# Masking the value product's blocks in one packed VectorE step, with ScalarE and GpSimd spreading the parts

## The chip, the cores and the metric

The kernel runs on one core of a Trainium2 chip. The metric is the device time of one execution in microseconds (us). The median of three runs of the kernel before is 414.5 us (413.69 to 414.89). The profile is of one more execution.

The core's engines are TensorE (PE in the profile, with PEld for its weight loads), VectorE (DVE), ScalarE (ACT), GpSimd (POOL) and SyncE (SP), whose queue starts most of the DMA transfers. Each works through its own list of instructions in order, and they wait for each other by semaphores.

## The reference

One block of a network: a layer norm, then linear attention with 32 heads of 16 columns, and beside it a two-layer MLP on the same normalised rows; both results and the input are added. What matters here, with `S = 2048` rows and `D = 512`:

```python
xn = _layernorm(x)
q, k, v = split(xn @ wqkv)                 # 32 heads of 16 columns
pq, pk = phi(q), phi(k)                    # phi(t) = where(t > 0, t + 1, exp(t)) + 1e-6
kv  = einsum("bhsd,bhse->bhde", pk, v)     # one 16x16 block per head
z   = einsum("bhsd->bhd", pk)
num = einsum("bhqd,bhde->bhqe", pq, kv)
den = einsum("bhqd,bhd->bhq", pq, z) + 1e-6
attention = (num / den) @ wo
r = relu(xn @ w1 + b1)
out = x + attention + (r * r) @ w2 + b2
```

Everything is float32. The change concerns `kv`, of which only the 32 diagonal blocks of 16x16 exist.

## The kernel before

**Float32 in parts.** Nearly every matrix operand is written as a high part (a copy rounded to the type that TensorE takes, `fp32r`) and a low part (the operand less its high part). `split(h, l, src, eh, el)` (line 117) makes them: a copy on engine `eh`, line 111 when that is ScalarE, and then a subtraction on engine `el`, line 119. A product of two such operands is three matmuls: high by high, high by low, low by high (`PASSES`, line 124; `three`, line 127, matmuls at line 130; `product`, line 480, matmuls at line 484).

**The stages.** Rows are worked in tiles of 128 and bands of four tiles. First a loop over the 16 tiles normalises them, turns them, projects the keys, applies `phi`, and sums in four PSUM banks the product of the normalised rows and `phi(k)` (`kx`, line 385). After that, the kernel computes queries and MLP for two bands at a time, in two rounds (`n` at line 915); each round has a loop over steps `p` (line 1040) that works a fast matrix multiplication out of sums and differences of blocks (the tiles `T`, `S` and `aop`). The tiles `m` hold the attention matrix: per head the `kv` block times the rows of `wo`.

**The order.** Nothing is scheduled automatically: the order in which the program text issues instructions is the order on each engine. The hand-written tables `AT` and `AE` say where delayed steps go. DMA loads are held back until the buffer that they fill is released by the engine that reads it.

**The step that is changed** stands between the two stages. `values()` (line 879, called at line 969) multiplies the value weights `wvs` with `kxs` in 128 small matmuls of 32 columns (line 889). Each lands on 32 partitions, so that the bank `pkv` holds 16 blocks of 32x32, packed: partition group `g` (32 partitions) and column group `j` (32 columns) hold the block of columns `128 j + 32 g`. Such a block covers two heads, and only its two 16x16 diagonal blocks are wanted; `heads` is the mask, made on GpSimd at the start (lines 531 to 536) as a 128x128 matrix with ones in the 16x16 blocks on the diagonal.

What the attention matrix needs is a block-diagonal operand: for each `j`, 128 rows by 128 columns, with the block of group `g` at rows and columns `32 g`. So the tile `kv` (128x512) is cleared by GpSimd (line 882), and four VectorE steps (line 894, one for each `g`) multiply the packed blocks on 32 partitions by the mask and write them to their places. Then `kvt`, its high and low part, is made from the whole of `kv`, zeros included: a ScalarE copy of 128x512 (line 111) and a VectorE subtraction of 128x512 (line 119).

`kvt` is the stationary operand of `matrix(j)` (line 900), three matmuls for each `j`, into the banks `pm`. `matrix(0)` and `matrix(1)` are called at lines 1123 and 1124 in step `p = 0` of the first round, ahead of the third of its products; `matrix(2)` and `matrix(3)` follow at lines 1159 and 1187. Around `values()`, VectorE also makes the low parts of `aop` (line 119), `T` and `w2r` (line 122) and the block sums `S` (line 714), and adds products into `q` (lines 1073, 1161, 1053). ScalarE makes the high parts (line 111). The raw rows of `w2` come by DMA (line 206), and GpSimd copies parts of them (`w2r`, `w2q`, lines 210 and 214).

## Time and profile before

| | us |
|---|---|
| median of three runs | 414.5 |
| the profiled execution | 413.35 |
| its span, from the first to the last instruction | 411.6 |
| TensorE busy | 406.3 |
| VectorE busy | 311.2 |
| ScalarE busy | 264.9 |
| GpSimd busy | 58.7 |

The clock that TensorE was granted is 1.0 of full speed over the whole span.

In the profile a row of a timeline gives the start, the duration, the engine, the line of the program, the instruction, the tile written and the tiles read, the shape (partitions x elements) and how many neighbouring instructions of a kind are put together; in brackets stands how long the engine was idle before and what ended that. A matmul's row is longer than the distance to the next one, since matmuls overlap: the distance of the starts tells what one costs. Tile names come without their numbers: `b` stands for all four banks of the products, `aop`, `T` and `S` for their operands, `pm` for the banks of `matrix`, and `w2r` and `r` for the parts and the raw rows of `w2`.

### The profile page before, as it was taken

Reading aid. Unit: us, or ns where it says so; the run is one execution under the profiler, and the core shown is the slowest. Engines: PE = TensorE matmul, PEld = TensorE weight load, DVE = VectorE, ACT = ScalarE, POOL = GpSimd, SP = SyncE. Lnnn points to the kernel's source line nnn. Section 1 sums busy time; section 2 is a strip of 40 time slices with the busy share of each in tenths; the row PEclk is TensorE's granted clock in tenths of the full one; section 3 lists DMA queues with packets and bytes.
Section 4 is the critical chain, followed back from the end, with each engine's and each line's share of the span. In section 5 each row is a group of like instructions: output and inputs, shape, how many; then the busy total and the mean of one; then the engine's idle time right before and its main releaser. Section 6 shows DMA issues by size and latency. Waiting matters only on the chain.

```text
span 411.6 us, 5590 instructions
## 1 busy us (share of the span) xinstructions
PE 406.3 (99%) x1927; PEld 334.0 (81%) x1927; DVE 311.2 (76%) x558; ACT 264.9 (64%) x465; POOL 58.7 (14%) x92
## 2 busy tenths in 40 slices
PE   8999999999999999999999999999999999999996
PEld 7788888888878888888878888888888888878885
DVE  5885666797899898988449995567989686449843
ACT  4666677656768779788638631577588857737520
POOL 4442333220310000030000130100000200001210
PEclk9999999999999999999999999999999999999999
DMA  6969672810422221273366992411121871024502
GB/s 213 343 217 337 195 307 103 246 36 0 118 64 68 87 76 52 79 201 55 133 239 236 401 166 90 116 51 53 51 76 29 236 186 37 0 101 156 102 2 102
DMA packets 45662, 55.16 MB, mean 134 GB/s; under 512 B 8001, under 2 KB 29761, under 8 KB 44354
## 3 DMA queue, kind: packets, MB, share of 16 engines
q1 hardware_dynamic: 43330, 50.61, 37.1%
q0 software_dynamic: 2304, 4.20, 6.3%
q8 instruction: 15, 0.25, 0.2%
q14 instruction: 13, 0.11, 0.1%
HBM read 41.43 MB, written 13.37 MB: 133 GB/s over the span
## 4 chain that ended last, share of the span: by engine, by line
PE 70%; DVE 3%; issue 1%; ACT 0%
PE acc L130 37%; PE b L484 30%; PE acc L495 2%; DVE T L122 1%; PE b L130 1%; PE pz L130 1%; DVE aop L119 1%; PE acc L502 0%; DVE S L714 0%; DVE w2r L122 0%; PE end L130 0%; DVE kvt L119 0%; ACT kvt L111 0%; DVE q L1053 0%; DVE q L1161 0%
## 5 line engine op out<-in xcount | busy, mean ns | idle before, releaser
L130 PE MATMUL acc<-w2r,s 128*128 128x512 f32 x477 | 112.8, 390 | 0.0
L130 PEld LDWEIGHTS acc<-w2r,s 128*128 128x128 f32 x477 | 89.4, 188 | 19.2 <-issue 0.7
L484 PE MATMUL b<-T,aop 128*128 128x512 f32 x336 | 84.0, 390 | 0.4 <-ACT T L111 0.2
L484 PEld LDWEIGHTS b<-T,aop 128*128 128x128 f32 x336 | 62.8, 188 | 14.7 <-ACT T L111 0.6
L385 PE MATMUL kx<-pk,tok 128*128 128x512 f32 x192 | 46.5, 391 | 0.1
L385 PEld LDWEIGHTS kx<-pk,tok 128*128 128x128 f32 x192 | 35.8, 188 | 7.9 <-ACT pk L111 0.5
L1021 POOL DMA_DIRECT2D res<-in_B_b_dram x16 | 14.4, 1089 | 180.5 <-DVE dt L426 64.2
L484 PE MATMUL b<-xs0h,aop 128*128 128x512 f32 x112 | 36.9, 390 | 0.0
L130 PE MATMUL acc<-mh,aTsr 128*128 128x512 f32 x112 | 35.6, 389 | 0.0
L1029 DVE TENSOR_TENSOR res<-acc,res 128x512 f32<-128x512 f32 x16 | 11.0, 692 | 23.1 <-PE acc L130 18.5
L119 POOL TENSOR_TENSOR tok<-xp,tok 128x512 fp32r<-128x512 f32 x16 | 20.7, 1298 | 43.4 <-ACT tok L111 43.4
L122 DVE TENSOR_TENSOR w2r<-r,w2r 128x512 fp32r<-128x512 f32 (+2 forms) x35 | 25.6, 734 | 0.1
L111 ACT ACTIVATE aop<-S 128x512 fp32r<-128x512 f32 x28 | 17.5, 624 | 11.7 <-DVE S L714 11.7
L484 PEld LDWEIGHTS b<-xs0h,aop 128*128 128x128 f32 x112 | 21.0, 188 | 4.4
L130 PEld LDWEIGHTS acc<-mh,aTsr 128*128 128x128 f32 x112 | 21.0, 188 | 4.4
L119 DVE TENSOR_TENSOR aop<-S,aop 128x512 fp32r<-128x512 f32 x28 | 19.5, 698 | 4.8 <-ACT aop L111 4.4
L119 DVE TENSOR_TENSOR s<-c,s 128x512 fp32r<-128x512 f32 x20 | 13.6, 690 | 11.0 <-ACT s L111 11.0
L484 PE MATMUL b<-xs0l,aop 128*128 128x512 f32 x56 | 21.8, 389 | 0.0
L130 PE MATMUL acc<-ml,aTsr 128*128 128x512 f32 x56 | 21.8, 389 | 0.0
L111 ACT ACTIVATE w2r<-r 128x512 fp32r<-128x512 f32 x32 | 19.6, 619 | 2.3 <-DMA out_dram<-res 2.0
L111 ACT ACTIVATE T<-Tf 128x512 fp32r<-128x512 f32 x16 | 9.5, 626 | 16.4 <-DVE Tf L657 16.1
L484 PE MATMUL b<-xs1h,aop 128*128 128x512 f32 x56 | 19.5, 389 | 0.0
(196 smaller groups left out, 765.0 us busy)
## 6 DMA issues: line engine op xcount, KB each, us to landing
r<-in_B_w_dram SPq DMA_DIRECT2D x49, 256.0 KB, 3.0
res<-in_A_x_dram SPq DMA_DIRECT2D x8, 512.0 KB, 4.6
res<-in_B_b_dram POOLq DMA_DIRECT2D x16, 256.0 KB, 5.5
out_dram<-res SPq DMA_DIRECT2D x15, 256.0 KB, 2.0
via<-xp SPq DMA_DIRECT2D x5, 512.0 KB, 3.0
xg<-via SPq DMA_DIRECT2D x20, 128.0 KB, 2.6
xTd<-t SPq DMA_DIRECT2D x8, 256.0 KB, 4.4
x<-in_A_x_dram SPq DMA_DIRECT2D x4, 512.0 KB, 8.1
```

Of the source, the lines that this page charges most:

```text
L111: nc.scalar.activation(o, i, AF.Copy, bias=bias)
L119: ENG[el].tensor_tensor(out=l, in0=src, in1=f32(h), op=OP.subtract)
L122: nc.vector.tensor_tensor(out=l, in0=src, in1=f32(h), op=OP.subtract)
L130: nc.tensor.matmul(ps, lhsT=a[u], rhs=b[v], start=first and n == 0, stop=last and n == 2)
L385: nc.tensor.matmul(kxp[c], lhsT=tok[i][:, u, c * P:(c + 1) * P], rhs=pk[i][:, v], start=i == 0 and (u, v) == first, stop=i == NT - 1 and ( ...
L484: nc.tensor.matmul(ps, lhsT=a[u][:, j * P:(j + 1) * P], rhs=b[v][:, j, :], start=first and j == 0 and n == 0, stop=last and j == 1 and n == 2,
L495: nc.tensor.matmul(ps, lhsT=s[u][:, k * P:(k + 1) * P], rhs=w2s[NF - 1][u][:, a:z], start=first and u == 0, stop=stop and u == 1)
L1021: nc.gpsimd.dma_start(r[:, i], b2[None, :].partition_broadcast(P), accum_op=OP.add)
L1029: nc.vector.tensor_tensor(out=r[:, a:z], in0=ps, in1=r[:, a:z], op=OP.add)
```

## The change

`values()` no longer writes the masked blocks to a cleared 128x512 tile. One VectorE step multiplies the packed 128x128 product by the mask, which is repeated over the four column groups, and leaves it packed. For that the mask's four 32x32 diagonal blocks have to lie in the first 32 columns: three small GpSimd copies at the start put them there. The cleared tile is now `kvt` itself, 128 partitions by 1024 elements, in two halves for the high and the low part. For each group of 32 partitions, ScalarE copies the four blocks into their places in the high half, and GpSimd subtracts and writes the low half. The VectorE subtraction over 128x512 is gone.

```diff
@@ -534,6 +534,9 @@
                                 pattern=[[-sign * (D // H), P * H // D], [0, D // H]],
                                 channel_multiplier=sign)
+    for k in range(1, NJ):
+        rows = slice(32 * k, 32 * (k + 1))
+        nc.gpsimd.tensor_copy(heads[rows, :32], heads[rows, rows])
     groups = {}
@@ -878,8 +881,9 @@
     def values():
         ps = bank("pkv", "acc")
-        t = w512("kv", "p", 6)
-        nc.gpsimd.memset(t, 0.0)
+        t = w512("kv", "p", 6)[:, :P].rearrange("p (j d) -> p j d", j=NJ)
+        kvt[0] = work.tile([P, 2, 512], F32R, name="kvt", tag="r3")
+        nc.gpsimd.memset(f32(kvt[0]), 0.0)
         R = 32
@@ -889,13 +893,12 @@
+        nc.vector.tensor_tensor(out=t, in0=ps[:, :P].rearrange("p (j d) -> p j d", j=NJ),
+                                in1=heads[:, None, :R].to_broadcast([P, NJ, R]), op=OP.mult)
         for g in range(NJ):
             rows = slice(R * g, R * (g + 1))
-            nc.vector.tensor_tensor(out=t[rows].rearrange("p (j d) -> p j d", j=NJ)[:, :, rows],
-                                    in0=ps[rows, :P].rearrange("p (j d) -> p j d", j=NJ),
-                                    in1=heads[rows, rows][:, None, :].to_broadcast([R, NJ, R]), op=OP.mult)
-        kvt[0] = work.tile([P, 2, 512], F32R, name="kvt", tag="r3")
-        split(kvt[0][:, 0], kvt[0][:, 1], t, "act", "dve")
+            h, l = (kvt[0][rows, u].rearrange("p (j d) -> p j d", j=NJ)[:, :, rows] for u in range(2))
+            split(h, l, t[rows], "act", "pool")
```

## The prediction

> **What bounds the kernel now.** I read the page first, then the busy time in stretches, then the chain of waits, then each engine's timeline around the change. All times are microseconds from the start of the span.
>
> The first fence is from the page: busy time, and the chain that ended last by engine.
>
> ```profile
> PE 406.3 (99%) x1927; PEld 334.0 (81%) x1927; DVE 311.2 (76%) x558; ACT 264.9 (64%) x465; POOL 58.7 (14%) x92
> ...
> PE 70%; DVE 3%; issue 1%; ACT 0%
> ```
>
> TensorE (PE) is busy for 99% of the span, so a change elsewhere earns only what PE now waits. Where is that? I cut the span into stretches (length, then busy time and count of PE, PEld, DVE, ACT, POOL):
>
> ```profile
> 103.50:119.70 16.20, 15.79 (x90) 12.32 (x76) 14.77 (x27) 11.41 (x23) 4.42 (x6) 1.00 0.40 116
> 119.70:408.20 288.50, 288.49 (x1283) 237.54 (x1283) 220.28 (x398) 187.05 (x326) 19.71 (x22) 1.00 0.38 112
> ```
>
> From 119.70 to 408.20 PE never waits: 288.49 of 288.50. In the stretch before it, which holds the changed step, VectorE (DVE) is busy 14.77 of 16.20. The chain of waits runs there:
>
> ```profile
> 104.57 1.91 issue
> 106.47 0.64 ACT kvt L111
> ...
> 107.14 0.69 DVE kvt L119
> ...
> 108.35 1.02 DVE aop L119 x2
> 109.37 1.01 DVE w2r L122
> ...
> 117.11 0.60 DVE q L1161
> 117.71 1.20 DVE T L122 x2
> 118.91 0.61 DVE q L1053
> ```
>
> So from 104.6 to 119.5 the chain is DVE's queue, and from 119.66 it is PE to the end. What PE loses in that stretch can be read from its starts:
>
> ```profile
> 107.86 1.53 PE L130 MATMUL pm<-wo,kvt 128*128 128x512 f32 x6
> 109.23 1.53 PE L484 MATMUL b<-T,aop 128*128 128x512 f32 x6
> ...
> 117.23 0.39 PE L484 MATMUL b<-xs0h,aop 128*128 128x512 f32 x1
> 117.86 1.63 PE L484 MATMUL b<-T,aop 128*128 128x512 f32 x6 [0.24 <-ACT T L111]
> 119.66 1.63 PE L484 MATMUL b<-T,aop 128*128 128x512 f32 x6 [0.17 <-DVE q L1053]
> 121.12 1.98 PE L495 MATMUL acc<-w2r,sz 128*128 128x512 f32 x8
> ```
>
> Six matmuls take 109.23 − 107.86 = 1.37, or 0.228 each. From 117.23 to 117.86 stands 0.63 where one matmul needs 0.23: 0.40 lost. From 117.86 to 119.66 stands 1.80 where six need 1.37: 0.43 lost. From 119.66 to 121.12 it is 1.46: 0.09 lost. **The cap on any gain downstream of the changed step is thus about 0.9 us**, however much DVE saves.
>
> **The change part by part.** It touches DVE, ScalarE (ACT) and GpSimd (POOL) between 105.2 and 108.7. DVE's timeline:
>
> ```profile
> 105.21 1.18 DVE L894 TENSOR_TENSOR kv<-pkv,heads 32x128 f32<-32x128 f32 x4
> 107.14 0.69 DVE L119 TENSOR_TENSOR kvt<-kv,kvt 128x512 fp32r<-128x512 f32 x1 [0.75 <-ACT kvt L111]
> 107.75 0.68 DVE L122 TENSOR_TENSOR T<-Tf,T 128x512 fp32r<-128x512 f32 x1
> 108.35 0.41 DVE L119 TENSOR_TENSOR aop<-rq,aop 128x256 fp32r<-128x256 f32 x1
> 108.69 0.68 DVE L119 TENSOR_TENSOR aop<-S,aop 128x512 fp32r<-128x512 f32 x1
> ```
>
> *DVE, removed:* three of the four L894 products (1.18 / 4 = 0.295 each), the idle 0.75 before the low part of kvt, and that subtraction, 0.61 to the next start. The new product has 128 columns over 128 partitions. The bounds are 0.295 (the same 128 columns on 32 partitions) and 0.41 (256 columns on all); I take the former, for its column count. So L894 ends at 105.50 and the T subtraction starts at about 105.45 and not 107.75: 2.3 earlier.
>
> *ACT:* one copy of 512 columns becomes four of 128.
>
> ```profile
> 106.47 0.63 ACT L111 ACTIVATE kvt<-kv 128x512 fp32r<-128x512 f32 x1 [1.91 <-issue]
> 107.01 0.40 ACT L111 ACTIVATE aop<-rq 128x256 fp32r<-128x256 f32 x1
> 107.32 0.61 ACT L111 ACTIVATE aop<-S 128x512 fp32r<-128x512 f32 x1
> ...
> 108.32 0.62 ACT L111 ACTIVATE w2r<-r 128x512 fp32r<-128x512 f32 x1
> ```
>
> Start to start, 512 columns take 0.52 and 256 take 0.31, so 128 take about 0.205 (ends 0.1 and 0.31), and one lasts 0.30. The first starts 0.08 after L894, as now, at 105.58; the four end at 105.88, 106.09, 106.29 and 106.50. The copy of aop<-rq starts at 106.40 (was 107.01) and aop<-S at 106.71: ACT gains 0.61. The w2r copy would come at 107.71 but needs its load. SP's timeline, and the DMA view of the same moments:
>
> ```profile
> 105.52 1.05 SPq L206 DMA_DIRECT2D r<-in_B_w_dram  x2
> ```
> ```profile
> r<-in_B_w_dram SPq DMA_DIRECT2D x2, 64.0 KB, 2.0
> ```
>
> The second of these begins about halfway, at 106.05, and lands 2.0 later, at about 108.1. It was released by a DVE step ahead of the change, so it doesn't move. So w2r starts at 108.1 and not 108.32, and ends at 108.72: **ACT keeps only 0.2 of its 0.61**. The low part of w2r on DVE (now 109.37 in the chain) then starts at about 108.78: a DVE gain of 0.5 to 0.6 survives that point. Of it the PE gaps at 117.86 and 119.66 can return 0.40 and then the rest.
>
> *POOL, added:* four subtractions of 32x128, each behind its ACT copy. No such row exists. The neighbours, from the groups by form and from POOL's timeline:
>
> ```profile
> L119 POOL TENSOR_TENSOR tok<-xp,tok 128x512 fp32r<-128x512 f32 x16 | 20.7, 1298 | 43.4 <-ACT tok L111 43.4
> ...
> L115 POOL CAST w2q<-w2r 32x512 fp32r<-32x512 f32 x4 | 3.5, 875 | 0.2
> ```
> ```profile
> 4.61 0.24 POOL L241 TENSOR_SCALAR y<-mv 128x1 f32<-128x1 f32 x1 [2.22 <-DVE mv L231]
> ```
>
> Lower end: a quarter of 1.30, 0.32. Upper end: 0.88, the w2q casts, POOL's only steps on 32 partitions. Taken: a fixed part of 0.24 (a step on a single column) and a quarter of the remaining 1.06: 0.50, and some 0.05 less from start to start, 0.45. I choose it for being nearest to tok's row, the same operation.
>
> When is the low part due? PE's weight loads of that product (matrix 0) and where they now stand:
>
> ```profile
> 107.86 0.42 PEld L130 LDWEIGHTS pm<-wo,kvt 128*128 128x128 f32 x2
> ```
>
> Each product makes three passes, high, high, low; the second of these two loads, one matmul spacing (0.23) behind the first at 108.09, is the first that needs the low part. Now it is ready at 107.83, 0.26 early. If PE waits here, everything on it moves by that wait, less the gaps of 0.9.
>
> *POOL beside DVE.* Two pairs of rows show what happens when both are busy; first POOL's, then DVE's of the same moments, a step with two SBUF inputs:
>
> ```profile
> 84.69 1.33 POOL L119 TENSOR_TENSOR tok<-xp,tok 128x512 fp32r<-128x512 f32 x1 [2.98 <-ACT tok L111]
> ```
> ```profile
> 84.79 1.78 DVE L679 TENSOR_TENSOR wv<-wv,wvl 128x512 f32<-128x512 f32 x1
> ```
> ```profile
> 109.90 3.66 POOL L115 CAST w2q<-w2r 32x512 fp32r<-32x512 f32 x4
> ```
> ```profile
> 112.04 2.06 DVE L122 TENSOR_TENSOR T<-Tf,T 128x512 fp32r<-128x512 f32 x2
> ```
>
> The DVE step that began 0.1 behind POOL took 1.78 and not 0.69: it ended 0.55 after POOL's did. In the second pair the DVE steps take 1.03 each and the casts 0.88 each: they alternate. So a new subtraction can hold up DVE, or wait for it. The T subtraction holds to about 106.06, so the first new one starts there (its ACT copy is ready at 106.02). Without any DVE step between, the four end at 106.06 + 3 × 0.45 + 0.50 = 107.9. DVE's next step, aop<-rq, is ready at 106.87 and takes 0.34 from POOL: 108.25. With the aop<-S step (0.61) let in too: 108.86. To this comes about 0.14, as now from w2r's end (108.94) to POOL's start (109.08). Due at 108.09, PE waits 0, 0.3 or 0.9. I take one step let in, 0.3: aop<-S becomes ready only when most of POOL's work is done.
>
> The Trainium skill, "SBUF — State Buffer", section "SBUF: two separate sides", says the same more strictly: the pair of ports is an exclusive lock for a whole instruction, against a DVE step with two SBUF inputs; this trace's 1.78 agrees. "GPSIMD Engine Reference", section "Engine selection", speaks against the change: two-input elementwise work is about twice as slow there as on VectorE. By that page a subtraction would be an estimated 0.59 (twice 0.295) and the low part would come some 0.4 later than by my 0.45 spacing; the 1.30 against 0.69 of this trace bears the ratio out.
>
> *Covered edits.* The cleared tile is now kvt, 1024 columns and not 512, and POOL can do it once the last tok step has ended:
>
> ```profile
> 96.14 0.53 POOL L882 MEMSET kv<- 128x512 f32 x1 [4.94 <-DVE pk L373]
> 109.08 0.76 POOL L115 CAST w2r<-w2r 64x512 fp32r<-64x512 f32 x1 [12.42 <-ACT w2r L111]
> ```
>
> It costs about 1.06 inside idle times of 4.9 and 12.4: nothing. The three copies of head blocks stand ahead of POOL's step at 4.61, before which it sits idle for 2.22. A copy's row:
>
> ```profile
> 8.24 0.18 POOL L591 COPY x<-xp 128x1 f32<-128x1 f32 x1
> ```
>
> Three at 0.18 to 0.32 (the quarter above) make 0.5 to 1.0, under the 2.22; without this cover they would delay the first tile by as much.
>
> **Sum.** DVE's queue reaches the end of the stretch 0.5 to 0.6 earlier; PE itself could come 0.9 − 0.3 = 0.6 earlier. The later of the two decides: a gain of 0.5. The profiled execution took 413.35 (span 411.6 and 1.75 around it), so 412.85; it lies 1.15 below the median of 414.5, so on the median **414.0**.
>
> **Rivals.** *All gaps close (413.6).* POOL's pieces overlap or cost 0.32, PE never waits for kvt, and w2r's load lands early enough: gain 0.9. For it: 0.40 and 0.43 are real gaps behind DVE. Against: the load at 108.1.
>
> *The wait moves to POOL (414.5).* Two DVE steps are let in, the low part is ready at 109.0, PE waits 0.9 and the gaps it had later pay for it: no gain, 414.3 to 414.8. For it: the strict alternation around 110 to 113. This is where the skill's exclusive lock leads if DVE's steps are always waiting. Against: DVE waits for ACT until 106.87.
>
> *The small subtractions are slow (415.3), the other side.* At the 0.88 of the w2q casts, the last ends at 106.06 + 3.5 = 109.6, is seen at 109.7, and PE stands 1.6 to 1.7 where it stood 0; the gaps give 0.9 back: 0.8 slower. It is slower from the point at which the low part comes after 109.0. If DVE is held as well and the gaps stay, up to 1.7: 416.2. Against: those casts had four times the columns and DVE's full steps in between.
>
> **How the numbers follow.** Forecast (gain of 0.3 to 0.7: 413.8 to 414.2) 0.45; all gaps close (413.4 to 413.8) 0.15; the wait moves (414.3 to 414.8) 0.28; slow subtractions (415.2 to 416.2) 0.12. The range from 413.3 to 415.2 leaves out the last and little more; its ends take in the 0.6 by which the three runs scatter about their median. A change of under 0.3%, 1.24 us, is about what a measurement of this kernel cannot tell from none. Faster by that exceeds the cap of 0.9: 0.04, for scatter alone. Slower by that, above 415.74, is half of the last case: 0.06. Within it: 0.90.
>
> **What would show it.** L894 as one step near 0.29; four ACT copies 0.2 apart; the T subtraction near 105.45; w2r's copy waiting for a DMA to 108.1; kvt's last subtraction ending near 108.2; the first pm product's third weight load at 108.1 to 108.6; the gaps at 117.2 and 119.2 shorter. The forecast is wrong if PE waits over 0.9 for kvt, if DVE's gain is lost to POOL before 117, or if PE shows idle time after 121 that it doesn't show now.

## The result, and the profile after

| | before | after |
|---|---|---|
| median (22 executions each) | 413.81 (412.80 to 414.95) | 412.88 (412.11 to 414.76) |
| the profiled execution | 413.35 | 412.76 |
| its span | 411.6 | 411.1 |

The ratio is 0.9978, with a 95% interval of 0.9968 to 0.9987: the change makes the kernel 0.9 us faster (0.54 to 1.32). The forecast was 414.0, in a range from 413.3 to 415.2, so the time lies below the range. Two things put it there. The forecast started from a median of three, 414.5, where 22 executions give 413.81; and it gave the change 0.5 where 0.9 was measured.

The page shows VectorE 1.0 less busy and GpSimd 3.8 more:

```profile
PE 406.3 (99%) x1927; PEld 334.4 (81%) x1927; DVE 310.2 (75%) x554; ACT 265.7 (65%) x468; POOL 62.5 (15%) x99
```

VectorE's timeline after, around the change (start, duration, engine, line, operation, tiles, shape, and in brackets its idle time and what ended it):

```profile
105.06 0.28 DVE L896 TENSOR_TENSOR kv<-pkv,heads 128x128 f32<-128x128 f32 x1
105.26 0.68 DVE L122 TENSOR_TENSOR T<-Tf,T 128x512 fp32r<-128x512 f32 x1
107.20 0.43 DVE L119 TENSOR_TENSOR aop<-rq,aop 128x256 fp32r<-128x256 f32 x1 [1.27 <-ACT aop L111]
...
108.72 1.71 DVE L122 TENSOR_TENSOR w2r<-r,w2r 64x512 fp32r<-64x512 f32 x2 [0.23 <-ACT w2r L111]
```

The packed product takes 0.28, the T subtraction starts at 105.26 and not at 107.75, and VectorE is now idle for 1.27 and 0.23 waiting for ScalarE. It reaches the low part of `w2r` at 108.72, where it was queued until 109.29 before. ScalarE's timeline of the same moments:

```profile
105.42 1.31 ACT L111 ACTIVATE kvt<-kv 32x128 fp32r<-32x128 f32 x4 [1.01 <-issue]
106.75 0.42 ACT L111 ACTIVATE aop<-rq 128x256 fp32r<-128x256 f32 x1
...
107.60 0.58 ACT L111 ACTIVATE c<-b 128x512 f32<-128x512 f32 x1
108.08 0.62 ACT L111 ACTIVATE w2r<-r 128x512 fp32r<-128x512 f32 x1
```

The four copies stand (106.75 − 105.42) / 4 = 0.33 apart. The `w2r` copy follows `c<-b` by 0.48, as it did before (107.84 to 108.32), and its row names no wait. GpSimd's row for the low part:

```profile
105.81 2.14 POOL L119 TENSOR_TENSOR kvt<-kv,kvt 32x128 fp32r<-32x128 f32 x4 [13.64 <-ACT kvt L111]
```

The low part of `kvt` is complete at 105.81 + 2.14 = 107.95, with the pieces 0.53 apart. The three copies of `heads` (0.70 together, at 2.47) and the clearing of `kvt` (0.95, at 91.22) stand far ahead of it. TensorE's timeline:

```profile
107.70 1.53 PE L130 MATMUL pm<-wo,kvt 128*128 128x512 f32 x6
109.07 1.53 PE L484 MATMUL b<-T,aop 128*128 128x512 f32 x6
...
117.05 0.39 PE L484 MATMUL b<-xs0h,aop 128*128 128x512 f32 x1
117.28 1.61 PE L484 MATMUL b<-T,aop 128*128 128x512 f32 x6
119.08 1.63 PE L484 MATMUL b<-T,aop 128*128 128x512 f32 x6 [0.19 <-DVE q L1056]
```
```profile
120.55 1.99 PE L495 MATMUL acc<-w2r,sz 128*128 128x512 f32 x8
```

From 107.70 to 109.07 stand 1.37 for six matmuls: TensorE does not wait for `kvt`. From 117.05 to 117.28 stand 0.23, so the first gap of 0.40 is closed. From 117.28 to 119.08 stand 1.80 for six, as before: the second gap, 0.43, is still there. The chain of waits runs through VectorE's queue from `w2r` to this addition:

```profile
108.72 0.68 DVE w2r L122
...
118.33 0.61 DVE q L1056
```

To compare profiles whose starts are shifted, I use the **stage**: the time from the start of the `pkv` matmuls to the start of those of L495. Before it runs from 102.35 to 121.12, 18.77; after from 102.20 to 120.55, 18.35. So the change earns 0.42 here. Of the 0.59 between the two profiled executions the other 0.15 lies ahead of the stage (102.35 against 102.20); in five profiles of the unchanged kernel the first matmul of `pkv` starts anywhere from 101.85 to 102.86, so that part is scatter.

The 0.42 has a history on VectorE. Counted from the start of `pkv`, it reaches the low part of `w2r` 0.41 earlier than before, at 6.53 and not at 6.94. There its two steps take 1.71 where they took 2.11: before, GpSimd's cast of `w2r` had started first (109.08 against 109.29), and now VectorE's step does (108.72 against 108.83). The same two cases stand in every profile in which the order can be seen: 2.11 to 2.13 in the five where GpSimd starts first, 1.71 in the twelve where VectorE does. So VectorE is 0.81 ahead at its next addition (8.27 and not 9.08). Then it meets one more of GpSimd's `w2q` casts, which end at the same 113.6 as before, and gives 0.41 back. The low part of `aop` after, and then before:

```profile
113.04 1.09 DVE L119 TENSOR_TENSOR aop<-r,aop 128x512 fp32r<-128x512 f32 x1
```
```profile
114.03 0.68 DVE L119 TENSOR_TENSOR aop<-r,aop 128x512 fp32r<-128x512 f32 x1
```

Behind the stage the 0.42 is kept. The first matmuls of `acc<-w2r,s` (L130), some 12 behind those of L495, start 30.37 after those of `pkv` before (132.72 − 102.35) and 29.94 after (132.14 − 102.20), 0.43 less. I call this the **long stage**; from its end to the end of the span every profile of either kernel and its variants takes 278.9.

The 22 executions say more than 0.42, however. Over many executions those of the kernel before pile up around 412.9 and around 414.1, with fewer between. Here and below I call those above 413.5 late and count them. In the kernel before 16 of 22 do, and 102 of the 155 that were timed beside all the runs of this study; in the changed kernel 3 of 22, and 5 of 34 with its second measurement. A fixed mark favours a kernel that is faster throughout: moved down by the stage's 0.42 it counts 9 of the 34, which is still far fewer. The medians of the executions up to 413.5 are 413.20 and 412.82, 0.38 apart, near the stage's 0.42. The rest of the 0.9 is that late executions became rarer. What the late ones lose is the second question of the experiments.

### The profile page after: what moved, and what is told of

It reads as the page before. It is cut to its first block, busy times and chain, and to the rows that moved or that the text cites. A ratio compares the mean times of both kernels' runs of the same rounds, so it can differ in the third digit from the quotient of the medians.

```text
span 411.1 us, 5600 instructions
## 1 busy us (share of the span) xinstructions
PE 406.3 (99%) x1927; PEld 334.4 (81%) x1927; DVE 310.2 (75%) x554; ACT 265.7 (65%) x468; POOL 62.5 (15%) x99
## 4 chain that ended last, share of the span: by engine, by line
PE 92%; DVE 3%; ACT 2%; DMA 1%; issue 1%; POOL 0%; POOLq 0%
PE acc L130 37%; PE b L484 30%; PE pk L365 11%; PE kx L385 10%; PE acc L495 2%; PE pz L130 1%; DVE T L122 1%; PE b L130 1%; DMA x<-in_A_x_dram 1%; PE pt L304 1%; DVE aop L119 0%; DVE w2r L122 0%; ACT kxs L111 0%; ACT aop L111 0%; PE acc L502 0%
## 5 line engine op out<-in xcount | busy, mean ns | idle before, releaser
L130 PE MATMUL acc<-w2r,s 128*128 128x512 f32 x477 | 112.8, 390 | 0.0
L130 PEld LDWEIGHTS acc<-w2r,s 128*128 128x128 f32 x477 | 89.4, 188 | 19.3 <-issue 0.7
L130 PE MATMUL acc<-mh,aTsr 128*128 128x512 f32 x112 | 35.6, 389 | 0.0
L130 PEld LDWEIGHTS acc<-mh,aTsr 128*128 128x128 f32 x112 | 21.0, 188 | 4.4
L130 PE MATMUL acc<-ml,aTsr 128*128 128x512 f32 x56 | 21.8, 389 | 0.0
```

The lines of the kernel that those rows point to most:

```text
L130: nc.tensor.matmul(ps, lhsT=a[u], rhs=b[v], start=first and n == 0, stop=last and n == 2)
```

## The experiments

The theory after the result: VectorE's chain, from the low part of `w2r` to the additions into `q`, sets when TensorE gets past the two gaps, and the change brings it there 0.42 earlier. The rivals: the low part of `kvt` on GpSimd has become a limit; the GpSimd work at the start matters; the pieces' sizes are set by the spread destination; and, for the late executions, several causes that are taken up below. Each set of runs was timed on one chip beside executions of the kernel before, and the ratios compare within a set.

### The kernels again, as controls

c1_before is the unchanged kernel run as if it were a change, d1_after the changed one a second time; e4_before, f3_before and f4_before are single profiled executions of the kernel before.

> The kernel before, once more, timed against itself. Ratio 1.000; its interval shows what five rounds can tell. In its profile the two gaps of TensorE in the stage behind the value product stand as before: 0.63 us between the starts of the last b<-xs0h matmul and the first b<-T one (0.40 lost), and 1.80 us over the six b<-T matmuls (0.43 lost). If the first row statistics start at another time than 3.61, the whole trace is moved by that, and a part of the 0.5 us between the two spans was start-up scatter.

> After, once more. Theory A (VectorE's earlier arrival closes the first gap of 0.40 and nothing else): 0.4 to 0.6 us faster than before, ratio 0.9985 to 0.9990. Theory E (both kernels stand at the w2r copy when its rows land late; what a pair of runs shows depends on that landing): the ratio scatters from set to set between 0.996 and 1.000, and in the profile the addition q<-b,c of line 1164 follows the end of ScalarE's w2r copy by the same 7.7 to 7.8 us as in after (116.45 - 108.70).

> One more look at the kernel before. Its time is in one of two clusters, 412.6 to 413.3 or 413.9 to 414.5. Theory E: in the upper cluster ScalarE's w2r copy waits for a DMA and stage pkv to L495 takes about 20 us, in the lower one 18.8. If it is in the upper cluster with 18.8, the difference between the clusters lies elsewhere.

> A look at the kernel before, to catch a late execution. Theory E: if the time is above 413.5 us, ScalarE's w2r copy waits for a DMA and pkv to L495 takes 19.5 to 20.1 us. Otherwise the loss stands ahead of the value product, as the 1.16 us in e3_best for a transfer of x.

> The same once more: above 413.5 us with a wait of the w2r copy for a DMA (theory E), or with a loss elsewhere.

The control gave 1.0011 (0.9989 to 1.0034). The second measurement of the changed kernel gave 0.9973 (0.9955 to 0.9991), a median of 412.65, and a stage of 18.35 again. E4 took 412.89 with a stage of 18.79: an on-time execution has the same stage as the profile of before, to 0.02 (and a long stage of 30.39 beside 30.37). The profiles of c1 (414.28), f3 (414.08) and f4 (415.72) caught late executions, with stages of 20.09, 19.92 and 20.57. In c1, ScalarE's row and then TensorE's rows show what is late:

```profile
109.53 0.63 ACT L111 ACTIVATE w2r<-r 128x512 fp32r<-128x512 f32 x1 [1.54 <-DMA r<-in_B_w_dram]
```
```profile
113.72 1.67 PE L484 MATMUL b<-T,aop 128*128 128x512 f32 x6 [0.62 <-ACT c L111]
118.75 1.63 PE L484 MATMUL b<-T,aop 128*128 128x512 f32 x6 [0.53 <-ACT T L111]
120.55 1.63 PE L484 MATMUL b<-T,aop 128*128 128x512 f32 x6 [0.17 <-DVE q L1053]
```

ScalarE waits 1.54 for the raw rows of `w2`, everything behind it on ScalarE and VectorE is late, and TensorE pays for it in three places: the stage is 1.32 longer. F3 and f4 show the same: waits of 1.38 and 2.01 ahead of this copy. (F4 is late in a second place too: `pkv` starts at 102.86, 1.0 later than in e4.) The view of the loads gives the reason. In c1 the two loads of 64 KB take 3.7 from issue to landing where they took 2.0 in the profile of before:

```profile
r<-in_B_w_dram SPq DMA_DIRECT2D x2, 64.0 KB, 3.7
```

### What is left of the second gap

c2_sum_first takes the changed kernel and issues the addition of `t5` into `q` (L1056) ahead of VectorE's low parts of `T`, which TensorE doesn't need as soon.

```diff
-                last_sums(4, difference_high, difference_low)
+                last_sums(4, difference_high)
...
                 nc.vector.tensor_tensor(out=t5 if was == "w" else q[t2][:, pb], in0=before, in1=t5, op=OP.add)
+            if p == 1:
+                last_sums(4, difference_low)
```

> After, and the two low parts of the fourth sum T are made behind the addition of t5 on VectorE instead of ahead of it. Theory A (VectorE's queue releases TensorE's banks): the second gap closes too, since the addition q<-b,t ends 1.2 us earlier; six b<-T matmuls take 1.37 to 1.45 us and not 1.80, and the time falls by 0.35 to 0.45 us below after: ratio to before 0.9968 to 0.9978 if after is at 0.9978 by 0.9 us, 0.998 if after's own gain is the 0.42 of its stage. Rival B (TensorE waits there for the low parts or for ScalarE's sz): no change against after.

TensorE's rows:

```profile
116.96 0.39 PE L484 MATMUL b<-xs0h,aop 128*128 128x512 f32 x1
117.45 2.97 PE L484 MATMUL b<-T,aop 128*128 128x512 f32 x12
```

The twelve matmuls stand together, so the second gap is gone, and it was a matter of VectorE's order; 0.26 of the first came back (117.45 − 116.96 − 0.23). In this profile ScalarE waits 0.18 for the rows of `w2`, and VectorE comes to `w2r` 0.30 later than in the changed kernel (6.83 behind the start of `pkv`, and not 6.53). The stage is 18.19, 0.16 under the changed kernel's, where theory A had 0.35 to 0.45. None of it arrives: the long stage is 30.25 (132.31 − 102.06), 0.31 over the changed kernel's 29.94, about as much as those rows came late. The median of 413.01, with a ratio of 0.9982 (0.9964 to 1.0000), doesn't tell it from 412.88. So by this profile closing the second gap by another order earns nothing in the end.

### Is the low part on GpSimd the limit?

c3_low_dve gives the four low parts to VectorE; c4_low_thrice makes each of them three times on GpSimd.

```diff
-            split(h, l, t[rows], "act", "pool")
+            split(h, l, t[rows], "act", "dve")
```
```diff
             split(h, l, t[rows], "act", "pool")
+            nc.gpsimd.tensor_tensor(out=l, in0=t[rows], in1=f32(h), op=OP.subtract)
+            nc.gpsimd.tensor_tensor(out=l, in0=t[rows], in1=f32(h), op=OP.subtract)
```

> After, with the four low parts on VectorE and not on GpSimd. Theory A: VectorE waits for ScalarE's four copies (to 106.7) and is then 1.8 us later at the T subtraction than after, but it makes up most of that, as it then waits less for aop and w2r; its additions into q come 0.2 to 0.4 us later than in after, the first gap stays closed or nearly, the second grows: 0.1 to 0.4 us slower than after, 0.1 to 0.4 faster than before. Rival C (the gain is the leaving of VectorE altogether, so it is all lost): 0.4 to 0.5 slower than after, equal to before.

> After, with each low part made three times on GpSimd: twelve subtractions of about 0.52 us and not four, so that the last ends near 112 and not at 107.96. It shows what a late low part costs. Theory A: TensorE stands at the first product of matrix(0) from 107.9 until 112, about 4 us, and the gap of 0.43 that is left later gives at most that back: 3.2 to 4.0 us slower than after (ratio to before 1.006 to 1.0075). Rival D (TensorE finds other work or the wait is short, as the low part is used late): under 1 us.

C3 was expected to be 0.1 to 0.4 slower than the changed kernel, and it was not: median 412.89, ratio 0.9982 (0.9965 to 0.9999), stage 18.37, long stage 29.97. Its VectorE timeline says why:

```profile
105.71 1.29 DVE L119 TENSOR_TENSOR kvt<-kv,kvt 32x128 fp32r<-32x128 f32 x4 [0.42 <-ACT kvt L111]
...
108.68 1.71 DVE L122 TENSOR_TENSOR w2r<-r,w2r 64x512 fp32r<-64x512 f32 x2
```

The 1.29 that VectorE spends here it spent waiting in the changed kernel; it comes to `w2r` at 108.68 either way. So **the GpSimd half of the change earns nothing here**. What earns is on VectorE: one product of 0.28 in place of four of 1.18 together, and a wait of 0.42 in place of 0.75, against which the four low parts cost 1.29 where one of 0.69 stood.

C4 shows what it costs when the low part does come late. GpSimd's last piece ends at 113.73; TensorE's rows:

```profile
113.79 2.07 PE L130 MATMUL pm<-wo,kvt 128*128 128x512 f32 x4 [5.78 <-POOL kvt L903]
115.66 2.76 PE L484 MATMUL b<-T,aop 128*128 128x512 f32 x6
```

The ratio is 1.0174 (1.0138 to 1.0210) at a median of 420.82, twice the loss that was expected. The first four of GpSimd's twelve pieces start 0.53 to 0.62 apart, later ones up to 1.05, where they alternate with VectorE's steps. And TensorE, once it has its operand, is slow: the six matmuls from 115.66 take 2.56, to the start of the next ones at 118.22, and not 1.37. In the busy time by stretch (length, then busy time and count of PE, PEld, DVE, ACT and POOL, then the granted clock) it stands directly:

```profile
113.70:119.40 5.70, 5.61 (x14) 4.41 (x15) 2.13 (x6) 2.65 (x6) 3.07 (x6) 0.52 0.00 1
```

After 5.78 idle the clock is 0.52 of full speed for about 5.5. The rule for that stands in the Trainium skill, "TensorE: Matmul & The Clock Gate", section "What's actually happening": after an idle window of about 3.4 us the array gets half its clock, until it has been busy for at least one such window. The 0.52 agrees.

### What a piece costs by itself

d4_pieces computes nothing of the reference: it copies one tile of `x` to the output and beside that times blocks of 128 columns on ScalarE and GpSimd, eight of each kind one behind the other: on all partitions (`whole`), on one group of 32 (`same`), on groups that change from one to the next (`turns`), and with the destination spread over the four blocks, on one group (`still`) or on changing ones (`spread`).

```diff
+    for k in range(8):
+        act(same[one(k), k, :P], src[one(k), :P])
+    for k in range(8):
+        act(turns[group(k), k, :P], src[group(k), :P])
...
+    for k in range(8):
+        sub(gturns[group(k), k, :P], src[group(k), :P], low[group(k), :P])
```

> The costs by themselves: it computes nothing of the reference and writes a part of x over the whole output. Eight ScalarE copies of 128 columns each: on 128 partitions; on partitions 0 to 31; on the four groups of 32 in turn; into four blocks of 32 columns on one group; and so on the groups in turn, as in the change. Then the same on GpSimd as subtractions. Forecast's theory: 0.205 us from start to start on ScalarE in all. Rival F: copies that change the group of partitions don't overlap and take 0.33. Rival G: it is the spread destination that takes 0.33. GpSimd: 0.45 start to start in all by the forecast; 0.53 was seen in after.

Both engines' rows from the timeline:

```profile
5.54 1.69 ACT L71 ACTIVATE whole<-src 128x128 fp32r<-128x128 f32 x8
7.13 1.69 ACT L71 ACTIVATE same<-src 32x128 fp32r<-32x128 f32 x8
7.46 3.32 POOL L86 TENSOR_TENSOR gsame<-src,low 32x128 fp32r<-32x128 f32 x8
8.73 2.52 ACT L71 ACTIVATE turns<-src 32x128 fp32r<-32x128 f32 x8
10.75 3.98 POOL L86 TENSOR_TENSOR gturns<-src,low 32x128 fp32r<-32x128 f32 x8
11.26 1.70 ACT L71 ACTIVATE still<-src 32x128 fp32r<-32x128 f32 x8
12.87 2.52 ACT L71 ACTIVATE spread<-src 32x128 fp32r<-32x128 f32 x8
14.79 3.98 POOL L86 TENSOR_TENSOR gspread<-src,low 32x128 fp32r<-32x128 f32 x8
```

Take one duration (0.30 on ScalarE, 0.45 on GpSimd, from the groups) off the eight and divide by seven. ScalarE: 0.20 on all partitions and on one group, 0.32 on changing groups. GpSimd: 0.41 and 0.505. The spread destination costs nothing on either. So the prediction's 0.205 for ScalarE was right for a copy that stays on its partitions, and the 0.33 of the changed kernel comes with the change of group.

### GpSimd beside VectorE

The four `w2q` casts on GpSimd run against VectorE's steps at 110 to 114 (the prediction's alternation). d2_w2_late, with c2's order, moves both parts of `w2r` behind VectorE's additions into `q`; e1_q_late_before (the kernel before) and e2_q_late (the changed one) only put the four casts at the end of step `p = 1`.

```diff
+            if p == 1:
+                last_sums(4, difference_low)
+                if n == 0:
+                    next_2(0)
...
-                if n == 0 and p == 0:
-                    next_2(0)
...
-                last_sums(4, difference_high, difference_low)
+                last_sums(4, difference_high)
+                if n == 0:
+                    high_2()
```
```diff
-                    copy("pool", w2s["q"][k * Q:(k + 1) * Q], h[2 * Q:3 * Q])
+                    later_q.append(lambda k=k: copy("pool", w2s["q"][k * Q:(k + 1) * Q], h[2 * Q:3 * Q]))
...
+            if n == 0 and p == 1:
+                do(later_q, TB)
```

> After with t5 added ahead of the fourth T's low parts, and the w2r copy and its low parts moved behind the additions that release TensorE's banks. Theory E: VectorE and ScalarE no longer stand at the landing of the w2 rows, VectorE comes to the addition of line 1164 about 1.7 us earlier, both gaps are gone (12 b<-T matmuls in 2.97), and the time no longer depends on that landing: 0.8 to 1.3 us faster than before, ratio 0.9968 to 0.9980. If GpSimd's cast of w2r is late for the L495 matmuls, they wait up to 0.5 us. Theory A alone: no better than c2_sum_first.

> The kernel before, and GpSimd's four w2q copies, whose result is first read near 212 us, are made one step later, behind the third product of step p = 1. Theory A (what counts is when VectorE frees TensorE's banks): the low parts of T and aop no longer alternate with these copies, VectorE comes to the two additions of lines 1161 and 1053 about 1.0 to 1.2 us earlier, more than the masks' change gives (0.57), and TensorE's two gaps close (18.0 us or less from the start of pkv to the L495 matmuls, 18.77 before, 18.35 after): faster than before by 0.7 to 0.9 us, at least as fast as after. Rival H (the gain of the change is its own work leaving VectorE): no change to before, or 0.1 to 0.2 us.

> After, with the same delay of the w2q copies. Theory A: both gaps are closed already without the change, so after gains 0.4 us on itself and then equals e1_q_late_before within 0.2 us: with that delay the change is worth nothing in its stage. Rival H: 0.4 us or more faster than e1_q_late_before.

D2 closed both gaps (the twelve matmuls take 2.88 from 116.89) and opened another, so that of the 0.8 to 1.3 expected nothing was left: 0.9999 (0.9980 to 1.0018). The timelines of GpSimd and of TensorE:

```profile
116.23 4.01 POOL L115 CAST w2q<-w2r 32x512 fp32r<-32x512 f32 x4
120.30 0.95 POOL L115 CAST sz<-sz 64x512 fp32r<-64x512 f32 x1
```
```profile
121.30 1.90 PE L495 MATMUL acc<-w2r,sz 128*128 128x512 f32 x7 [1.30 <-POOL sz L115]
```

The cast of `sz`, which TensorE needs, now stands behind the four casts. E1 and e2 keep it ahead of them. E1, which has nothing of the change, shows

```profile
116.66 0.39 PE L484 MATMUL b<-xs0h,aop 128*128 128x512 f32 x1
116.89 2.98 PE L484 MATMUL b<-T,aop 128*128 128x512 f32 x12
119.70 1.98 PE L495 MATMUL acc<-w2r,sz 128*128 128x512 f32 x8
```

Both gaps are closed, with a stage of 17.93 (from 101.77) and a median of 413.11, 0.9983 (0.9969 to 0.9997). E2 has 17.85, 412.48 and 0.9978 (0.9965 to 0.9992). In the stage, then, the changed step seems worth only 0.08 beside the delayed casts. But the stage ends too early to tell. Behind it the casts stand in VectorE's way again. E1's VectorE, GpSimd and TensorE, and the start of `acc<-w2r,s` in the kernel before:

```profile
118.12 1.09 DVE L122 TENSOR_TENSOR sz<-r2c,sz 64x512 fp32r<-64x512 f32 x1
...
122.12 1.49 DVE L122 TENSOR_TENSOR sz0q<-r2c,sz 32x128 fp32r<-32x128 f32 x4
```
```profile
118.72 3.86 POOL L115 CAST w2q<-w2r 32x512 fp32r<-32x512 f32 x4
```
```profile
130.53 1.66 PE L484 MATMUL b<-T,aop 128*128 128x512 f32 x6 [0.23 <-DVE t L1053]
132.03 2.88 PE L130 MATMUL acc<-w2r,s 128*128 128x512 f32 x12
```
```profile
132.72 2.88 PE L130 MATMUL acc<-w2r,s 128*128 128x512 f32 x12
```

Those two VectorE rows took 0.69 and 1.17 before. From the start of L495 to that of `acc<-w2r,s` e1 takes 12.33 where the kernel before takes 11.60: most of what the closed gaps gave is lost again.

| | stage | long stage | gain in the long stage |
|---|---|---|---|
| before | 18.77 | 30.37 | |
| after | 18.35 | 29.94 | 0.43 |
| e1_q_late_before | 17.93 | 30.26 | 0.11 |
| e2_q_late | 17.85 | 29.52 | 0.85 |

So the delayed casts alone leave 0.11 in this profile, the change alone 0.43, and both together 0.85: beside the delayed casts the changed step is worth more, not less. The executions up to 413.5 say the same of e1: their median is 412.56, and 412.77 for the kernel before in the same set. By the long stage this is rival H of the two expectations, 0.1 to 0.2 for e1 and e2 at least 0.4 faster than that: what earns in the end is the work that left VectorE, whose queue still holds TensorE up at 130. In e1's profile the rows of `w2` were somewhat late (ScalarE waits 0.55 for them, and VectorE comes to `w2r` 0.34 later than before), but as VectorE's step on `w2r` then starts ahead of GpSimd's cast, it is back in place at the next addition (9.02 behind the start of `pkv`, and 9.08 before). The times alone don't decide, since the intervals of the two ratios overlap.

### The late executions

Which part of the change makes them rarer? f1_pool_start puts only the change's early GpSimd work (the three copies of `heads` and the clearing of `kvt`) into the kernel before. d3_zc_later (on the changed kernel) and f2_zc_later_before issue four small loads (`zc`, line 875) behind those of `w2` on SyncE's queue, and so the `w2` loads earlier. g1_rq_early_before moves the small split of `aop<-rq` ahead of `kvt`'s.

```diff
+    for k in range(1, NJ):
+        rows = slice(32 * k, 32 * (k + 1))
+        nc.gpsimd.tensor_copy(heads[rows, :32], heads[rows, rows])
...
+        kvt[0] = work.tile([P, 2, 512], F32R, name="kvt", tag="r3")
+        nc.gpsimd.memset(f32(kvt[0]), 0.0)
```
```diff
-    of_g = zd.rearrange("o (g j c) -> g c (o j)", g=NJ, j=NJ)
-    for k in range(NJ):
-        nc.sync.dma_start(zc[32 * k:32 * (k + 1), 0], of_g[k])
...
             w2next = piece_2(NF - 1, 0)
+            of_g = zd.rearrange("o (g j c) -> g c (o j)", g=NJ, j=NJ)
+            for k in range(NJ):
+                nc.sync.dma_start(zc[32 * k:32 * (k + 1), 0], of_g[k])
```
```diff
+        extra.pop(1)()
         kvt[0] = work.tile([P, 2, 512], F32R, name="kvt", tag="r3")
         split(kvt[0][:, 0], kvt[0][:, 1], t, "act", "dve")
```

> The kernel before, with what the change adds on GpSimd ahead of the value product and nothing else: the three copies of head blocks at the start, and kvt cleared early (it is then written over as before). Theory A says that these are idle time: the stage from pkv to the L495 matmuls takes 18.8 us, and the time is that of before, ratio 1.000 with 0.002 to either side, over half of the runs above 413.5 us. Rival B (the late executions are rarer with the change because GpSimd's work at the start moves the first transfers or steps): ratio 0.998, under a third of the runs above 413.5.

> After, and the four small zc loads, for which SyncE's queue waits until zd has landed, are issued behind the three loads of the last w2 rows instead of ahead of them. Theory E: these rows are issued at about 103.5 and land by 107; ScalarE's w2r copy follows its queue at 108.0 in every run. The profile is as in after; the time is 0 to 0.6 us below after, for the runs in which the rows now land late. Theory A: no change against after.

> The kernel before, with the small zc loads issued behind the three loads of the last w2 rows, so that these rows are under way earlier. Theory E (before's late executions are those in which the w2 rows land late, as in c1_before): under a third of the runs is above 413.5 us, and the ratio is 0.9975 to 0.9985, without any of the change. If the late ones have another cause: ratio 1.000, over half above 413.5.

> The kernel before, with the small split of aop<-rq (256 columns) issued behind the four L894 products and ahead of kvt's split; nothing else is changed and nothing left out. Its ScalarE copy falls into the idle 1.91 before 106.47 and its VectorE subtraction into the idle 0.75 before 107.14, so the raw buffer that it reads is released at about 106.9 and not at 108.8, earlier than in the changed kernel (107.6), while the change itself is absent. In the stage from the start of the pkv matmuls to that of L495, VectorE has 0.34 less behind 108.35, so 18.4 to 18.6 and not 18.77 (w2r's copy still ends at 108.9). Theory S, the SyncE stall is the cause of the late executions: SyncE's wait for VectorE's aop<-rq goes, the w2 rows land in time nearly always, at most 25% of the executions lie above 413.5, the median is 412.6 to 413.0 and the ratio 0.997 to 0.999. Theory N, the stall only goes along with the late rows: 50% or more above 413.5, a median of 413.5 to 413.8, a ratio of 0.999 to 1.000.

| | stage | median | ratio (95%) | above 413.5 |
|---|---|---|---|---|
| f1_pool_start | 18.78 | 413.81 | 1.0003 (0.9983 to 1.0023) | 7 of 12 |
| d3_zc_later | 18.35 | 412.59 | 0.9972 (0.9956 to 0.9988) | 3 of 12 |
| f2_zc_later_before | 18.77 | 412.95 | 0.9987 (0.9970 to 1.0005) | 3 of 12 |
| g1_rq_early_before | 18.44 | 413.26 | 0.9993 (0.9974 to 1.0012) | 6 of 12 |

Twelve executions tell little of a share: c1, the unchanged kernel, had 10 of 12 above 413.5. F1 looks like the kernel before. In f2 the share is small with the stage unchanged, which is what earlier `w2` loads should do; SyncE's timeline has them at 100.96 and not at 104.14. On the changed kernel the same move (d3) earned nothing that can be told: 412.59, and 412.65 without it in the same set.

```profile
100.96 1.62 SPq L206 DMA_DIRECT2D r<-in_B_w_dram  x3
```

Its two 64 KB loads took 3.4 to land, about as long as in the late executions, but from an earlier start that does no harm. So that late rows of `w2` cost 1.2 to 1.8 of the stage is shown in c1, f3 and f4 by the waits, and that they make executions late is borne out by f2's share, though f2's interval takes in 1.

They are not the only source. The profile of e3 (below) took 413.44 without any wait for `w2`; its `pkv` starts at 103.38, behind a wait in the first loop:

```profile
51.38 0.50 PE L365 MATMUL pk<-wkh,xs1h 128*128 128x512 f32 x1 [1.16 <-ACT xs1h L320]
```

ScalarE had waited there for VectorE's turning of a tile, and VectorE 4.5 for a load of rows (`xg<-via`). G2's profile (413.53) shows the same with 0.91, f4's with 0.35, and the on-time profiles of before and after show no wait at this place. How many of the late executions come from here is not known.

Why do the rows need 2.0 in one execution and 3.7 in another, and why is that rarer with the change? In the three late profiles SyncE's load of line 184 stalls behind VectorE for 1.0 to 1.5 (in the on-time profile of before the stalls are at lines 206 and 165). In the first profile of the changed kernel only 0.5 is left of them, at line 206 (in d1 1.2 and 0.2): VectorE's subtraction of `aop<-rq` ends at 107.63 and not at 108.76, and so releases its raw buffer earlier. G1 was to take the stall away without the change. It did shorten the stage, by 0.33 as expected, but not the stall. SyncE's waits in it:

```profile
SPq L165 <- DVE T L122: 0.9, 1, 0.9
SPq L184 <- DVE aop L119: 0.4, 1, 0.4
```

The load now waits for VectorE's next step, and 6 of 12 are late. That fits the theory that the stall goes along only, but since the stall stayed, it doesn't decide. It speaks against the stall as the cause that in the late profiles it stands behind the `w2` loads on SyncE's queue, and that f2, whose `w2` loads went out earlier, was on time with a stall of 1.7 at line 184. **The cause of the slow landing, and so of the second half of the gain, stays open.**

### The best of it

e3_best joins c2's, d3's and e2's moves on the changed kernel; g2_best_rq_early adds g1's.

```diff
-                last_sums(4, difference_high, difference_low)
+                last_sums(4, difference_high)
...
+            if n == 0 and p == 1:
+                do(later_q, TB)
...
+            for k in range(NJ):
+                nc.sync.dma_start(zc[32 * k:32 * (k + 1), 0], of_g[k])
```
```diff
                                 in1=heads[:, None, :R].to_broadcast([P, NJ, R]), op=OP.mult)
+        extra.pop(1)()
```

> After, with the w2q copies late, t5 added ahead of the fourth T's low parts, and the small zc loads issued behind the w2 rows. Theory A: the gaps can be closed only once, so it is no better than e2_q_late in its fast runs (18.0 us or less from pkv to L495). Theory E: it has slack for late landings, so fewer of its runs are above 413.6 us than of after (4 of 22): a median of 412.2 to 412.5 beside 413.9 of before.

> The changed kernel with all three moves of e3_best (w2q casts late, the t5 addition ahead of the low parts, the small zc loads behind those of w2) and with the aop<-rq split issued right behind the packed product. E3 had a median of 412.19. PE's two gaps are closed there already, so the stage stays at 17.8 to 17.9 and the time at 412.0 to 412.4 unless GpSimd's low part of kvt is held up by the VectorE subtraction that now stands in its way: then the third weight load of pm waits 0.1 to 0.4, and what stands behind it moves by no more than the slack of VectorE there, 412.2 to 412.6. Under theory S the share of executions above the lower cluster is as small as in e3 or smaller; theory N says nothing of it.

E3 has a median of 412.19 (ratio 0.9966, 0.9954 to 0.9979), a stage of 17.87, 0.5 under the changed kernel's, and a long stage of 29.49, within 0.03 of e2's; 1 of 12 lies above 413.5. It is the fastest version of the study, 1.7 under the median of before in the same set (413.90). G2 gave 412.46 (0.9970, 0.9952 to 0.9988) with a stage of 18.38, in the band that was expected if GpSimd is held up. Its GpSimd and TensorE rows show that case:

```profile
106.84 2.70 POOL L119 TENSOR_TENSOR kvt<-kv,kvt 32x128 fp32r<-32x128 f32 x4 [13.44 <-ACT kvt L111]
```
```profile
108.73 0.62 PE L130 MATMUL pm<-wo,kvt 128*128 128x512 f32 x2
109.59 1.19 PE L130 MATMUL pm<-wo,kvt 128*128 128x512 f32 x4 [0.24 <-POOL kvt L119]
```

VectorE's steps stand closer to GpSimd's pieces here, the four take 2.70 and not 2.14, and TensorE waits: 109.59 − 108.73 − 2 × 0.23 = 0.40. This is the prediction's "wait for kvt", in a kernel where VectorE comes earlier.

## Why the prediction was wrong, point by point

- **The sum on the median failed first.** The step "on the median 414.0" took 414.5 from three executions as the level. Of 22 it was 413.81, and of the 155 in this study 413.96. Executions fall into two groups about 1.3 apart (medians 412.92 and 414.25 of the 155, below and above 413.5), and all three happened to lie in the upper one. With 413.81 as the level the same gain makes 413.3, and the range, moved along by 0.69, would have taken in the 412.88 that was measured. The range's lower end, 413.3, allowed only 0.6 for such scatter.
- **The gain was taken as one figure for every execution.** The forecast of 0.5 in the profiled execution was near: the stage gave 0.42, and the median went down by 0.9 because 3 of 22 executions are late now instead of 16 of 22. The prediction took the landing of the `w2` load as fixed at 2.0. This was the term that varied, 2.0 to 3.7, and one profile couldn't show it. The profiled execution, at 413.35 below all three timed ones, was a hint. How the change makes late executions rarer stays open.
- **The 0.42 was near by a different route**, and so partly by luck. The forecast had VectorE 0.5 to 0.6 ahead at the low part of `w2r` and lost nothing behind it. It was 0.41 ahead there, 0.81 ahead one addition later, and gave 0.41 back to GpSimd's casts.
- **The cap of 0.9 held, but "PE never waits" behind 119.70 was read from busy time**, where rows of 0.39 that start 0.23 apart cover small waits. The starts show them: in the profile of before those of 130.87, 131.23 and 131.57 stand 0.36 and 0.34 apart. VectorE's queue still matters there. E1 and e2, with both gaps closed, earned 0.84 and 0.92 in the stage (18.77 less 17.93 and 17.85), and of that e1 kept 0.11 at the end of the long stage.
- **VectorE's side was right**: L894 became one step of 0.28 (0.295 forecast), and the T subtraction started at 105.26 (105.45).
- **ScalarE's copies were mis-sized**: 0.33 apart and not 0.205, and d4 shows that the change of partition group is what costs. So ScalarE gained 0.26 and not 0.61 up to `aop<-rq` (107.01 to 106.75). It made no difference to the sum, as the prediction had ScalarE wait for the `w2` load until 108.1 anyway. The copy did start at 108.08, but directly behind `c<-b`: a right figure by a wrong wait.
- **GpSimd's pieces were mis-sized too**, 0.53 apart and not 0.45, from the same cause (0.505 against 0.41 in d4). Against this, the wait for one VectorE step was counted at 0.34; in c4, where the pieces show singly, the fourth took 0.55 beside VectorE's step and not 0.45, so it cost 0.1. The low part was complete at 107.95, and the third weight load follows at 108.01. That load is 0.07 behind its usual spacing of 0.23 (107.71 + 0.23 = 107.94), so it did wait for the low part, but its matmul still starts on time. The forecast wait of TensorE, 0.3, didn't come.
- **The later of the two decides** was the right rule, and it was VectorE's arrival: the first gap closed, the second stayed at 0.43, as c2 and e1 explain.
- **The rivals.** "All gaps close" failed in the changed kernel for lack of VectorE's time, and e2 reaches it, 0.85 at the end of the long stage. "The wait moves to POOL" didn't happen, with nothing to spare, and happened in g2. "The small subtractions are slow" needed 0.88 a piece; it was 0.53. None of the rivals gave a gain through rarer late executions.

## What to carry to other kernels

- Before a forecast is put on a median, look at how the executions scatter. If they fall into groups, a change of half a microsecond moves the median by what it does to the shares, and the profile of one execution shows one group only.
- When a waiting engine's queue is shortened, see what can fill the freed time: here VectorE could have made the low parts itself for nothing, because it waited for ScalarE's `w2r` either way.
- A closed gap is not yet a gain. Delaying GpSimd's casts took 0.84 out of the stage by itself and left 0.11 in this profile, because they collided with VectorE's later steps; together with the change it left 0.85. Follow the bounding queue to the place from which all versions take the same time.

## What the runs showed of the hardware that was not expected

- Consecutive steps on **changing groups of 32 partitions** cost more than on one group or on all 128: 0.32 against 0.20 on ScalarE and 0.505 against 0.41 on GpSimd, for 128 columns. The Trainium skill, "GPSIMD Engine Reference", section "Instruction dispatch", says that each of GpSimd's cores serves its own 16 partitions and starts the next instruction as soon as its own share of the last is done. From that one would expect pieces on changing groups to follow closer, if anything; these rows show them farther apart, and the rows decide.
- One wait of 5.78 on TensorE cost some 2.1 more in the matmuls behind it (c4: 4.43 from 113.79 to 118.22 for ten, and not 2.28).
- Loads of 64 KB by one queue landed 2.0 after their issue in some executions and 3.4 to 3.7 in others of the same kernel or its near kin.
- Which of two engines starts first, by 0.1 or 0.2, decided which one was held. Where VectorE's step on `w2r` started ahead of GpSimd's cast (108.72 against 108.83 after the change) it took 0.68 and the cast 1.05; where it started behind (109.29 against 109.08 before) it took 1.09 and the cast 0.76.
